# Thirteen of 24 normalizations moved to GpSimd in an attention-plus-gated-MLP kernel whose order is written out by hand

## The chip, the core and the metric

The kernel runs on one core of a Trainium2 chip. The core has TensorE (matrix products; in the profile PE, and PEld for the loading of its stationary operand), VectorE (DVE), ScalarE (ACT), GpSimd (POOL) and SyncE (SP, which here only issues DMAs). The four compute engines and the DMA queue run independently, each through its own instruction list in order, and wait for each other through semaphores. SBUF is the on-chip memory, PSUM holds eight banks of TensorE results; GpSimd does not read PSUM in this kernel.

The metric is the time of one execution in microseconds, as the device measures it. A profiled execution gives, beside its time, the span from the first to the last instruction and a trace of every instruction.

## The reference: what is computed

Two parts follow each other. The first is linear attention with decay over 4 batches, 8 heads, 768 positions and 64 columns a head, in blocks of 64 positions:

```python
intra = np.einsum('bhic,bhjc->bhij', qb, kb) * Dmask[None]
intra = np.einsum('bhij,bhjd->bhid', intra, vb)
inter = np.einsum('bhid,bhde->bhie', qb * lam_pow[None], kv_state)
out[:, :, sl] = intra + inter
kv_state = lam_block[None, :, None, None] * kv_state + np.einsum('bhsd,bhse->bhde', kb_dec, vb)
```

Its output, with the heads side by side, is x (4 x 768 x 512). The second part is a gated MLP with a spatial product over the 768 positions:

```python
h = np.maximum(x @ w_in, 0.0)
u, v = (h[..., :d_ff // 2].copy(), h[..., d_ff // 2:].copy())
v_n = (v - mu) / np.sqrt(var + 1e-06)          # mu, var over the 512 columns of v
v_s = np.einsum('ts,bsd->btd', w_spatial, v_n) + b_spatial[None, :, None]
gated = u * v_s
return (gated @ w_out).astype(np.float32)
```

Inputs and the output are float32; the products run in bfloat16.

## The kernel before

The 768 positions of a batch are cut into three steps of 256, so there are twelve steps, 0 to 11; batch b has steps 3b to 3b+2. There are no loops over time in the program: a string ORDER of 717 tokens is read from left to right, and each token issues the instructions of one operation. A token is a name, its numbers and the engine: T is TensorE, D VectorE, A ScalarE, P GpSimd, S the DMA queue of SyncE. `VN.7.1.P` normalizes the second half of step 7 on GpSimd. Only the order of the tokens of one engine among themselves matters, since each engine works off its own list; last numbers of many tokens name PSUM banks. Dependencies (data, and buffers that become free) are turned into semaphore waits by the framework.

One step n goes through these operations:

- Loads: LQ, LK, LV bring 512 KB each of q, k, v into one of three input buffers.
- Scaling: QM and KM multiply halves of q and k by powers of the decay into bfloat16 (line 331), VC and VD cast v.
- Transposes of q and k: by TensorE for steps 0 to 5 (TQ, TK, line 366, copied out of PSUM by EQ, EK), by transposing DMAs on the queue for steps 6 to 11 (DQ line 348, DK line 344).
- Attention: SC makes the scores (line 396), MK masks them into SBUF on VectorE (401), KP adds to the running state (425), SX, SY, SA copy and add state (431 to 441), AV makes the output (459, 468) in two parts. Between the parts stands FN, a copy of one element that keeps the second part behind the first. EX copies the result out as xT, the MLP's input.
- The v half: PV (493, four matmuls), EV with the ReLU (498, 500), BN the statistics (508, 509), RA the square root on ScalarE, RD the reciprocal and RB a product on VectorE, VN the normalized v_n (526 to 533). RB is needed only by ScalarE's form of VN.
- The u half: PU (544, eight matmuls) and EU with the ReLU.

When the three steps of a batch have their v_n and u, the spatial product follows: GP writes the bias into a PSUM bank, PW adds the product of v_n and the transposed W_spatial (570, six matmuls over the six 128-row pieces s of the batch; v_n of step n and half c is piece 2(n mod 3) + c), GM multiplies by u (576), PO and PH make the output product (581, 590), EO and EH copy it to SBUF, ST and SH store it.

The weights arrive in float32 during the first 45 us through staging buffers: WH and CW, CX for w_in; WQ (load of one 128-row piece), WC (cast), WT (six transposes on TensorE), EW (copy out of PSUM) for W_spatial; WP and WX for w_out. The staging buffers of w_in are used again: WQ.0 and WQ.1 wait for CW, WQ.4 and WQ.5 for CX. FL are matmuls of ones that fill TensorE's waits at the start; LB, LN, LL, LX make the table of decays; BB and BE spread the bias.

VN takes its engine from the token:

```python
def v_n(e, n, c):
    t, p2 = 2 * (n % NR) + c, n // NR % 2
    if e == "A":
        nc.scalar.activation(out=vn[p2][:, t], in_=vh[p2][:, t], func=AF.Identity,
                             scale=rstd[p2][:, t:t + 1], bias=nmr[p2][:, t:t + 1])
        return
    vec(e).tensor_scalar(out=vn[p2][:, t], in0=vh[p2][:, t], scalar1=mv[p2][:, t, 0:1],
                         scalar2=rstd[p2][:, t:t + 1], op0=ALU.subtract, op1=ALU.mult)
```

Of the kernel before, what the change touches and what calls it, by code (L numbers as in the profile page):

```python
# [17 lines left out]
one.D row.D FL.1.256.3.1.T FL.2.256.0.1.T FL.1.256.1.1.T LB.0.T FL.2.256.1.1.T FL.1.256.1.1.T FL.2.256.2.1.T
FL.2.256.5.1.T BB.1.6.T BB.0.1.T LN.0.A LL.D LX.A KM.0.1.D QM.0.0.P FL.1.256.0.1.T TQ.0.0.4.T QM.0.1.D KM.0.0.D
TQ.0.1.3.T TK.0.0.2.T TK.0.1.5.T FL.2.256.0.1.T EQ.0.0.4.D mkc.D EQ.0.1.3.D EK.0.1.5.D QM.1.1.D QM.1.0.P BE.0.1.A  # L20
BE.1.6.A EK.0.0.2.A tab.1.A SC.0.0.1.2.T MK.0.0.1.2.D VC.0.P KP.0.4.T SC.0.1.5.6.T TQ.1.0.0.T KM.1.0.P KM.1.1.P
# [60 lines left out]
EH.3.5.0.0.D ST.1.4.S SH.3.5.0.S ST.2.5.S GM.3.3.0.6.D GM.3.0.0.2.D PO.3.0.1.T PH.3.5.1.3.T PO.3.2.0.T EH.3.5.1.3.A
SH.3.5.1.A PO.3.1.6.T EO.3.1.6.A EO.3.3.5.D ST.3.3.S EO.3.4.4.D ST.3.4.S EO.3.0.1.D ST.3.0.S EO.3.2.0.D ST.3.2.S
ST.3.1.S
"""


# [556 lines left out]
```

## Time and profile before

| what | value |
|---|---|
| median of 3 runs | 143.06 us (142.86 to 143.22) |
| the profiled execution | 142.01 us |
| its span, first to last instruction | 140.3 us |
| mean granted TensorE clock | 0.995 |
| busy: TensorE / VectorE / ScalarE / GpSimd | 132.7 / 114.3 / 80.1 / 55.6 us |
| read from and written to HBM | 24.38 MB, 6.29 MB |

The profiled execution has 1.7 us around its span. "Busy" is the union of an engine's instructions; matmuls are pipelined and their ends modelled, so a busy TensorE row is not one at its peak. A row of the chain of waits is: start, length, what; a row of the timeline is: start, length, engine, line, operation, what is written and read, shape, count, and in brackets the idle time before it with what ended it. In the groups by line, the two numbers behind the bar are the busy time of the group and the mean nanoseconds of one instruction. L12 is line 12 of the kernel.

### The profile page before, as it was taken

The page shows a single profiled execution, that of the slowest core. Times are in us where ns is not written, and L with a number is a line of the kernel's source. Part 1 is how long each engine was busy: PE and PEld are TensorE (multiplying, and loading weights), DVE is VectorE, ACT ScalarE, POOL GpSimd, SP SyncE. Part 2 cuts the span into 40 slices and gives each one's busy share as a digit, 9 for nine tenths or more (in the row PEclk, how much of TensorE's full clock was granted, in tenths as well). Part 3 has the DMA queues.
Part 4 walks back from the last instruction along what each step waited for, and adds up shares of the span by engine and source line. Part 5 has one row for each costly group of instructions (what it writes and reads, how often), then busy time and mean ns, then how long its engine had stood idle before and what let it go on. Part 6 is the DMA issues. An engine that isn't in the chain of part 4 may idle for free.

```text
span 140.3 us, 4712 instructions
## 1 busy us (share of the span) xinstructions
PE 132.7 (95%) x1984; PEld 86.4 (62%) x1998; DVE 114.3 (81%) x229; ACT 80.1 (57%) x160; POOL 55.6 (40%) x64
## 2 busy tenths in 40 slices
PE   5999799999999999999999999999999999999990
PEld 3478574778567657648656456586555645866540
DVE  2299799979999998999488799779899799986660
ACT  4168488799667577359532278696124476962011
POOL 5268655842397459800861409701930000000000
PEclk9999999999999999999999999999999999999998
DMA  3999999999999999998917799999986980000174
GB/s 79 346 346 347 386 376 345 336 374 360 361 349 322 297 314 289 335 201 196 276 27 67 170 343 310 328 193 200 287 281 79 355 315 12 0 2 0 41 296 186
DMA packets 56729, 34.12 MB, mean 243 GB/s; under 512 B 13827, under 2 KB 51971, under 8 KB 56708
## 3 DMA queue, kind: packets, MB, share of 16 engines
q1 hardware_dynamic: 56560, 33.69, 84.4%
q8 instruction: 15, 0.25, 0.7%
q10 hardware_dynamic: 148, 0.13, 0.3%
q14 instruction: 6, 0.05, 0.1%
HBM read 24.38 MB, written 6.29 MB: 219 GB/s over the span
## 4 chain that ended last, share of the span: by engine, by line
PE 78%; SPq 6%; DMA 5%; DVE 3%; ACT 2%; issue 2%; POOL 1%; ACTq 0%; POOLq 0%
PE ps L570 22%; PE ps L581 14%; PE ps L493 14%; PE ps L544 13%; SPq L196 6%; DMA q_in<-in_q_dram 5%; PE ps L468 4%; PE ps L396 3%; PE ps L459 3%; PE ps L425 2%; PE ps L366 2%; POOL qc L331 1%; DVE vn L532 1%; ACT uT L498 1%; PE ps L556 1%
## 5 line engine op out<-in xcount | busy, mean ns | idle before, releaser
L570 PE MATMUL ps<-wt_sb,vn 128*128 128x384 bf16 x192 | 33.2, 326 | 0.2 <-DVE vn L532 0.2
L401 DVE TENSOR_TENSOR a_sb<-ps,m 128x1024 bf16<-128x1024 f32 x24 | 28.7, 1216 | 1.8 <-PE ps L396 1.3
L570 PEld LDWEIGHTS <-vn 128*128 128x128 bf16 x192 | 18.3, 98 | 12.1 <-DVE vn L532 0.6
L331 POOL TENSOR_TENSOR qc<-q_in,lqn 128x512 bf16<-128x512 f32 x18 | 19.4, 1093 | 15.4 <-DMA q_in<-in_q_dram 7.9
L544 PE MATMUL ps<-xT,win_sb 128*128 128x256 bf16 x192 | 23.1, 273 | 0.0
L493 PE MATMUL ps<-win_sb,xT 128*128 128x512 bf16 x92 | 22.5, 379 | 0.3 <-issue 0.2
L581 PE MATMUL ps<-wout_sb,gT 128*128 128x512 bf16 x82 | 21.3, 380 | 0.6 <-issue 0.2
L576 DVE TENSOR_TENSOR gT<-ps,uT 128x384 bf16<-128x384 f32 x32 | 16.7, 550 | 5.7 <-PE ps L570 5.6
L544 PEld LDWEIGHTS <-win_sb 128*128 128x128 bf16 x192 | 18.4, 98 | 3.9
L331 POOL TENSOR_TENSOR kc<-k_in,lv 128x512 bf16<-128x512 f32 x18 | 19.3, 1090 | 3.0 <-DMA k_in<-in_k_dram 2.6
L181 ACT ACTIVATE o_sb<-ps 128x512 f32<-128x512 f32 (+1 forms) x16 | 9.2, 580 | 17.4 <-PE ps L581 9.9
L508 DVE BATCH_NORM_STATS2 st<-vh 128x6 f32<-128x512 bf16 x24 | 16.4, 684 | 1.5 <-ACT vh L498 1.2
L181 ACT ACTIVATE ps<-bsp 128x384 f32<-128x384 f32 x23 | 11.1, 488 | 8.4 <-DVE gT L576 7.6
L181 ACT ACTIVATE xT<-ps 128x512 bf16<-128x512 f32 x23 | 12.5, 592 | 5.3 <-PE ps L468 5.1
L493 PEld LDWEIGHTS <-xT 128*128 128x128 bf16 x96 | 9.0, 98 | 9.5 <-ACT xT L181 1.3
L581 PEld LDWEIGHTS <-gT 128*128 128x128 bf16 x92 | 8.5, 98 | 9.1
L185 POOL CAST vb<-v_in 128x1024 bf16<-128x1024 f32 (+1 forms) x9 | 8.4, 941 | 12.6 <-DMA v_in<-in_v_dram 5.8
L498 ACT ACTIVATE vh<-ps 128x512 bf16<-128x512 f32 x18 | 10.5, 593 | 3.2 <-PE ps L493 3.2
L396 PE MATMUL ps<-qT,kT 64*64 64x128 bf16 x384 | 10.0, 226 | 1.1 <-issue 1.1
L468 PE MATMUL ps<-a_sb,vb 64*64 64x128 bf16 x384 | 9.9, 217 | 0.0
L498 ACT ACTIVATE uT<-ps 128x512 bf16<-128x512 f32 x16 | 9.2, 589 | 0.3 <-PE ps L544 0.3
L396 PEld LDWEIGHTS <-kT 64*64 64x64 bf16 x384 | 6.9, 111 | 2.8 <-issue 2.3
(77 smaller groups left out, 171.3 us busy)
## 6 DMA issues: line engine op xcount, KB each, us to landing
q_in<-in_q_dram SPq DMA_DIRECT2D x12, 512.0 KB, 6.7
k_in<-in_k_dram SPq DMA_DIRECT2D x12, 512.0 KB, 6.5
v_in<-in_v_dram SPq DMA_DIRECT2D x12, 512.0 KB, 6.3
out_dram<-o_sb SPq DMA_DIRECT2D x23, 256.0 KB, 3.1
wst<-in_moe_w_in_dram SPq DMA_DIRECT2D x4, 512.0 KB, 8.4
wst<-in_moe_w_spatial_dram SPq DMA_DIRECT2D x4, 384.0 KB, 7.4
wst<-in_moe_w_out_dram SPq DMA_DIRECT2D x1, 1024.0 KB
wss<-in_moe_w_spatial_dram SPq DMA_DIRECT2D x2, 384.0 KB, 7.0
```

The source lines that it names most:

```text
L181: nc.scalar.activation(out=o, in_=i, func=AF.Copy)
L331: vec(e).tensor_tensor(out=dst[n % NCA][:, u].rearrange("p u m o d -> p o (u m) d"), in0=src[n % NIN].rearrange("p (o u) m d -> p o u m d" ...
L396: nc.tensor.matmul(out=pa[o][row(c), w, j], lhsT=kT[n % NTR][row(o), u, j, c * Q64:(c + 1) * Q64], rhs=qv(n, o, u, c), start=(w == 0 and j ...
L401: nc.vector.tensor_tensor(out=a_sb[n % NA][:, i].rearrange("p o w j x -> p o w (j x)"), in0=ps[:, b0:b1 + 1:b1 - b0].rearrange("p o (w y) ...
L468: nc.tensor.matmul(out=po[c ^ o][row(w), c, i], lhsT=vb[n % NCA][row(c), 4 * o + u, j, :], rhs=a[row(c), i, o, w, j, :], start=(r == 0 and ...
L493: nc.tensor.matmul(out=bank(b), lhsT=x[:, slot(c, g)], rhs=win_sb[:, g, DH:DFF], start=(g == 0), stop=(g == NCH - 1))
L498: nc.scalar.activation(out=o, in_=i, func=AF.Relu)
L508: nc.vector.bn_stats(out=st6[p2][:, t], in_=vh[p2][:, t])
L544: nc.tensor.matmul(out=pu[:, f2].rearrange("p (c x) -> p c x", c=2), lhsT=win_sb[:, g, f * P:(f + 1) * P], rhs=x[:, slot(0, g):slot(1, g) ...
L570: nc.tensor.matmul(out=bank(b)[:, 0:HW], lhsT=vn[bb % 2][:, s, f * P:(f + 1) * P], rhs=wt_sb[:, s, i * HW:(i + 1) * HW], start=False, stop ...
L576: nc.vector.tensor_tensor(out=gT[bb % 2][:, f, cols], in0=bank(b)[:, 0:HW], in1=uT[bb % 2][:, f, cols], op=ALU.mult)
L581: nc.tensor.matmul(out=bank(b), lhsT=gT[bb % 2][:, f, t * P:(t + 1) * P], rhs=wout_sb[:, f, :], start=(f == 0), stop=(f == NCH - 1))
```

## The change

Only the string ORDER differs; the functions are the same. The new string has the same 717 operations.

- Engines of VN: before 18 on VectorE and 6 on ScalarE; after 13 on GpSimd, 7 on VectorE, 4 on ScalarE. On GpSimd are VN.1.0 and 1.1 (batch 0), 3.0, 4.0 and 4.1 (batch 1), 6.0, 6.1, 7.0 and 7.1 (batch 2), 9.0, 9.1, 10.0 and 10.1 (batch 3).
- Other operations that change engine, as counts before and after. EK: ScalarE 6 to 2, VectorE 3 to 7. EQ: ScalarE 6 to 8, VectorE 3 to 1. EV: ScalarE 18 to 15. EU: ScalarE 16 to 18. EO: ScalarE 15 to 17. EW: ScalarE 4 to 2. CW: ScalarE 2 to 0, VectorE 1 to 2, GpSimd 1 to 2. CX: one of two from GpSimd to VectorE. KM: GpSimd 18 to 20. VD: GpSimd 2 to 0, ScalarE 0 to 2.
- Loads: v of step 0 is third (before: q of step 1). WQ.1, 0, 2, 3, 4, 5 follow each other; before, LV.3 stood between WQ.5 and WQ.3. LQ.3 stands ahead of WH.2. LK.8 and LV.7 are behind the first four transposing DMAs instead of ahead of them.
- The order of every engine is another one, TensorE's included: of U groups, AV, KP and PO most are shifted by a few places, and many PSUM banks have other numbers. The fillers are 32 in both; one now stands behind the last output product.

The lines that hold the front, the spatial product of batch 0 and that of batch 2 (cut):

```diff
-lam.A BR.A tab.0.A LQ.0.S LK.0.S LQ.1.S LV.0.S LK.1.S LV.1.S LK.2.S LQ.2.S WH.0.S WH.1.S posk.P msk.P idn.P eps.D
...
-TQ.2.0.5.T FL.1.256.0.1.T TQ.2.1.1.T SA.1.1.D MK.1.1.3.4.D EQ.2.0.5.D CW.0.D SA.1.0.D EK.2.1.6.A EK.2.0.2.A
-AV.1.0.6.3.T SC.2.0.4.5.T MK.2.0.4.5.D EQ.2.1.1.A LV.2.S WH.3.S WH.2.S LK.3.S FN.1.6.3.A CW.1.A SC.2.1.0.1.T
-AV.1.1.6.3.T CW.3.A PV.0.0.2.T PV.0.1.4.T CX.1.P MK.2.1.0.1.D EV.0.1.4.D EX.1.0.6.A EX.1.1.3.A PV.1.0.5.T PV.1.1.0.T
...
-RA.2.A EW.2.0.1.D RD.2.D VN.1.1.D VN.1.0.D VN.0.0.D VN.2.1.D VN.2.0.D EW.0.0.2.A EW.1.0.4.A PU.2.0.0.T WQ.5.S LV.3.S
...
-RA.7.A EV.8.0.1.A SY.9.3.A RD.7.D RD.6.D SX.9.D RB.6.D BN.8.0.D PV.8.1.0.T RB.7.D EO.1.2.5.A EV.8.1.0.A VN.7.1.D
-BN.8.1.D VN.7.0.A VN.6.0.A PU.7.1.6.T PU.8.1.3.T RA.8.A EU.7.1.6.A RD.8.D RB.8.D VN.6.1.D SA.9.1.D VN.8.1.A VN.8.0.D
...
+lam.A BR.A tab.0.A LQ.0.S LK.0.S LV.0.S LQ.1.S LK.1.S idn.P posk.P msk.P one.D row.D FL.2.256.3.1.T FL.1.256.2.1.T
...
+VD.1.0.A SY.0.5.D MK.0.1.3.4.D EK.1.0.1.D SA.0.1.D EK.1.1.0.D FL.1.256.5.1.T SC.1.0.4.5.T AV.0.0.6.2.T
...
+WH.1.S FL.1.256.5.1.T TK.2.0.4.T FL.2.256.5.1.T FL.2.256.5.1.T TQ.2.0.5.T EX.0.0.6.A EX.0.1.2.A MK.1.1.0.1.D
+AV.1.0.1.0.T TQ.2.1.6.T TK.2.1.2.T EQ.2.0.5.A FN.1.1.0.A LV.2.S SY.1.3.D EK.2.0.4.D SA.1.0.D EK.2.1.2.D eps.D
+AV.1.1.1.0.T SC.2.0.3.4.T CW.2.D CW.3.D EQ.2.1.6.A SC.2.1.5.6.T SA.1.1.D MK.2.1.5.6.D EX.1.0.1.A EX.1.1.0.A WH.3.S
+MK.2.0.3.4.D CX.1.D CW.1.P CW.0.P LQ.3.S WH.2.S LK.3.S WQ.1.S WQ.0.S WQ.2.S PV.0.1.2.T PV.0.0.0.T PV.1.1.1.T
...
+EU.1.0.3.D RD.1.D PU.0.0.6.T TK.3.2.1.T WC.2.A EU.0.0.6.A WQ.3.S WQ.4.S WQ.5.S LK.4.S LV.3.S LQ.4.S EK.3.2.1.D
+WT.2.0.3.T WT.0.0.5.T WT.1.0.6.T EW.0.0.5.D EW.1.0.6.D PU.2.0.1.T VN.0.0.A RA.2.A EW.2.0.3.A EU.1.1.0.A RD.2.D
+VN.2.1.D VN.2.0.D WC.4.A EU.2.0.1.A WC.3.D WC.5.D WP.S LV.4.S VN.1.0.P VN.1.1.P SC.3.1.5.6.T PW.0.3.0.4.T
+PW.0.0.0.2.T MK.3.1.5.6.D GM.0.3.0.4.D KM.4.1.P KM.4.0.P QM.4.0.P GP.0.1.0.0.A GP.0.2.0.1.A WT.1.1.3.T PW.0.1.0.0.T
+WT.0.1.5.T EW.1.1.3.A WT.2.1.4.T GM.0.0.0.2.D GP.0.3.1.6.D EW.0.1.5.D EW.2.1.4.D GM.0.1.0.0.D VC.3.A GP.0.1.1.2.A
+GP.0.2.1.0.D PW.0.2.0.1.T WX.1.P GM.0.2.0.1.D KP.3.3.T SC.3.0.4.5.T PW.0.1.1.2.T PW.0.2.1.0.T GP.0.0.1.1.A SY.3.3.A
...
+LK.10.S LV.10.S KM.9.0.P KM.9.1.P GN.5.0.P DK.9.S ST.0.0.S ST.1.4.S KM.10.1.P VC.9.P LQ.11.S LK.11.S LQ.10.S DQ.9.S
...
+MK.8.0.5.6.D BN.6.0.D AV.8.0.0.3.T EV.7.1.4.A FN.8.0.3.D KP.9.1.T AV.8.1.0.3.T EX.8.0.0.A BN.7.0.D BN.7.1.D
+EX.8.1.3.A BN.6.1.D PO.1.2.6.T PV.8.0.0.T PV.8.1.5.T PU.7.1.4.T RA.7.A EV.8.0.0.D RD.7.D GP.2.3.0.3.A SY.9.1.A
...
+PU.7.0.6.T PU.8.1.1.T PU.8.0.5.T GP.2.2.0.0.A RD.8.D RB.8.D VN.8.1.D GP.2.2.1.4.D RB.7.D VN.8.0.A EU.8.1.1.A
+SA.9.1.D EU.8.0.5.D RB.6.D VN.7.1.P VN.6.0.P VN.6.1.P VN.7.0.P PW.2.2.0.0.T GM.2.2.0.0.D GP.2.0.0.1.D EU.7.0.6.A
+PW.2.1.1.2.T GM.2.1.1.2.D GP.2.3.1.5.A GP.2.1.0.0.A GP.2.0.1.6.A KM.10.0.P KM.11.0.P DK.10.S QM.11.1.P QM.11.0.P
+QM.10.0.P PW.2.3.0.3.T QM.10.1.D DQ.10.S PW.2.1.0.0.T PW.2.0.0.1.T PW.2.2.1.4.T GM.2.1.0.0.D GM.2.3.0.3.D KM.11.1.P
...
```

More of the change, by code (lines that the diff above doesn't have):

```diff
@@ L16 @@
 ORDER = """
-lam.A BR.A tab.0.A LQ.0.S LK.0.S LQ.1.S LV.0.S LK.1.S LV.1.S LK.2.S LQ.2.S WH.0.S WH.1.S posk.P msk.P idn.P eps.D
[L18 to L21, printed above, removed]
@@ L82 @@
[L82 to L84 removed]
+lam.A BR.A tab.0.A LQ.0.S LK.0.S LV.0.S LQ.1.S LK.1.S idn.P posk.P msk.P one.D row.D FL.2.256.3.1.T FL.1.256.2.1.T
+FL.4.256.0.1.T FL.1.256.6.1.T LB.2.T FL.2.256.6.1.T FL.2.256.3.1.T LN.2.A FL.1.256.1.1.T BB.0.5.T BB.1.3.T mkc.D
+LL.D LX.A KM.0.1.P QM.0.1.D QM.0.0.D TQ.0.0.0.T TK.0.1.6.T KM.0.0.D TK.0.0.4.T TQ.0.1.2.T BE.0.5.D BE.1.3.A
```

100 lines of the change are left out of this document (46 added, 54 removed).

## The prediction

> **What bounds the kernel now.** I read the profile's page first, then the chain that ended last in order of time, then the timeline around the places where the chain leaves TensorE. On the page, the span, busy times, granted clock, DMA share and rate in 40 slices:
>
> ```profile
> span 140.3 us, 4712 instructions
> ...
> PE 132.7 (95%) x1984; PEld 86.4 (62%) x1998; DVE 114.3 (81%) x229; ACT 80.1 (57%) x160; POOL 55.6 (40%) x64
> ...
> PEclk9999999999999999999999999999999999999998
> DMA  3999999999999999998917799999986980000174
> GB/s 79 346 346 347 386 376 345 336 374 360 361 349 322 297 314 289 335 201 196 276 27 67 170 343 310 328 193 200 287 281 79 355 315 12 0 2 0 41 296 186
> ```
>
> The clock is granted in full, so TensorE's time is its work and its waits. The chain in order of time (start, length, what):
>
> ```profile
> 9.30 7.37 DMA q_in<-in_q_dram
> ...
> 16.80 2.05 POOL qc L331 x2
> ...
> 20.89 3.40 PE ps L493 x15
> ...
> 43.88 0.45 PE ps L366 x8
> ...
> 58.11 0.17 ACT seen L181
> ...
> 90.98 4.37 PE ps L544 x40
> 95.35 5.85 PE ps L570 x36
> ...
> 136.73 0.60 ACT o_sb L181
> ```
>
> Until 16.8 us the chain waits for inputs (q of step 2 is the eighth load), GpSimd scales that q, and from the first V projection at 20.89 until 136.73 the chain is TensorE with small interruptions. The work is fixed: 0.109 us a U matmul (4.37 / 40), 0.1625 us a spatial one (5.85 / 36), 0.056 us a transpose (0.45 / 8). GpSimd is busy for 40% and VectorE for 81%, but neither sets the end. So taking v_n from VectorE (11 of them) and ScalarE (2) is worth only the TensorE waits that it ends. There are two candidates: the start of the V projections and the start of the spatial product. Behind them I allow nothing: the pause at 58.11 (a fence copy after AV.5.0) is still there, since again only KP stands between AV.5.0 and AV.5.1. The tail behind the last matmul (140.3 - 136.73 = 3.6 us) has the same last copy and the same last store; the filler matmul behind the last output product keeps nobody waiting.
>
> **The change part by part, first the front.** The timeline before the first V projection:
>
> ```profile
> 18.89 0.40 PE L366 MATMUL ps<-ident,qc 128*128 128x128 bf16 x4
> ...
> 19.09 0.42 DVE L183 CAST win_sb<-wst 128x512 bf16<-128x512 f32 x1
> 19.22 0.75 POOL L185 CAST win_sb<-wst 128x512 bf16<-128x512 f32 x1 [0.38 <-DMA wst<-in_moe_w_in_dram]
> ...
> 19.33 0.60 ACT L181 ACTIVATE qT<-ps 128x512 bf16<-128x512 bf16 x1 [0.22 <-PE ps L366]
> ```
>
> The view of DMA issues has, as the last column, the median us from issue to landing:
>
> ```profile
> v_in<-in_v_dram SPq DMA_DIRECT2D x12, 512.0 KB, 6.3
> ...
> qT<-qc SPq DMA_TRANSPOSE x6, 3.3
> ```
>
> The ten loads up to w_in's second V piece are the same set in both orders, so GpSimd's QM.2 pair (16.80 + 2.05 = 18.85) and TQ.2.1 (18.89) stay where they are. After that, before: AV.1.0, SC.2.0, the wait for EQ.2.1 (19.33 + 0.60 = 19.93), SC.2.1, AV.1.1, then PV. Changed: AV.1.0 is ahead of TQ.2.1, and TK.2.1 and AV.1.1 lie inside the wait for EQ.2.1. TK.2.1 starts 4 x 0.056 behind TQ.2.1 and, at 0.40 long like it, ends about 19.55; VectorE copies it (EK.2.1, about 0.4 as its cast at 19.09) until 20.0, SC.2.0 and SC.2.1 follow, and PV.0.1 can begin at 20.4: 0.45 us gained. The casts must keep up: GpSimd makes CW.1 and CW.0 from 18.85 (2 x 0.75, until 20.35), VectorE CW.2 and CW.3 from 20.0 (2 x 0.42, until 20.85; their data was there at 19.22, when GpSimd's cast stopped waiting); the matmul that reads CW.3 comes 3 x 0.22 behind 20.4, at 21.05. Bounds: 0.6 gained (PV right behind the copies) to 0.2 lost (casts late); I take 0.45.
>
> **The spatial product's start.** The timeline there, and one row of 20 us (ScalarE's last two casts):
>
> ```profile
> 19.88 1.13 ACT L181 ACTIVATE win_sb<-wst 128x512 bf16<-128x512 f32 x2
> ...
> 33.57 2.19 DVE L532 TENSOR_SCALAR vn<-vh,mv,rstd 128x512 bf16<-128x512 bf16 x5
> ...
> 34.43 0.87 POOL L185 CAST wsp_raw<-wst 128x768 bf16<-128x768 f32 x1 [2.47 <-DMA wst<-in_moe_w_spatial_dram]
> ...
> 34.81 0.82 PE L570 MATMUL ps<-wt_sb,vn 128*128 128x384 bf16 x4
> ...
> 35.82 2.45 PE L570 MATMUL ps<-wt_sb,vn 128*128 128x384 bf16 x14 [0.19 <-DVE vn L532]
> ```
>
> Four matmuls run, the fifth waits: it could begin at 34.81 + 4 x 0.1625 = 35.46 and begins at 35.82, because VectorE makes five v_n in a row at the end (33.57 + 2.19 = 35.76). Changed: ScalarE makes v_n 0 and 1, GpSimd 2 and 3, VectorE 4 and 5. With the PE order 0.45 earlier, PW.0.3.0 is reached at 34.35. The same fifth matmul, which now needs VN.2.0 from VectorE, is due at 35.0. VectorE has taken on CX.1, one more cast of w_in and several PSUM copies (EK.2, EQ.3, EW.1.0) in this stage and given away four v_n, EV.0.0 and QM.3.1; adding its row durations from 20.0 on I get VN.2.0 done at about 34.6. So 0.36 is saved, and the next thing late is VN.2.0 itself with 0.4 in hand. Bounds: 0 (VectorE's queue 0.4 later than my sum) to 0.36; I take 0.36.
>
> What GpSimd needs for one v_n, no row shows. Its nearest rows:
>
> ```profile
> 1.82 0.64 POOL L234 TENSOR_SCALAR_AFFINE_SELECT mfull<-mfull 128x512 bf16<-128x512 bf16 x1
> ...
> 12.92 1.16 POOL L185 CAST vb<-v_in 128x512 bf16<-128x512 f32 x2
> ...
> 14.05 1.48 POOL L331 TENSOR_TENSOR kc<-k_in,lv 128x512 bf16<-128x512 f32 x1
> ```
>
> and in the groups by line those of v_n itself and of GpSimd's two-input product:
>
> ```profile
> L331 POOL TENSOR_TENSOR kc<-k_in,lv 128x512 bf16<-128x512 f32 x18 | 19.3, 1090 | 3.0 <-DMA k_in<-in_k_dram 2.6 <-PE ps L468 0.5
> ...
> L532 DVE TENSOR_SCALAR vn<-vh,mv,rstd 128x512 bf16<-128x512 bf16 x18 | 7.0, 431 | 0.0
> ...
> L529 ACT ACTIVATE vn<-vh,nmr,rstd 128x512 bf16<-128x512 bf16 x6 | 4.7, 816 | 0.0
> ...
> L500 DVE TENSOR_SCALAR vh<-ps 128x512 bf16<-128x512 f32 x6 | 4.0, 681 | 1.1 <-PE ps L493 1.1
> ```
>
> One input of 512 elements costs 0.58 to 0.64, two cost 1.09 and 1.48 at worst. v_n has one large input, so I take 0.64 and keep 1.48 as the other end. In batch 0 the two GpSimd v_n follow WC.0 and RD.1 (about 31.5 in my sum of VectorE's queue): even 2 x 1.48 ends at 34.5, and the fourth matmul is due at 34.85. KM.4 and QM.4 are queued behind them; their products are first transposed by TK.4 and TQ.4 beyond 42 us.
>
> **The later batches.** Batch 1's GpSimd v_n have over 3 us between RD.4 and PW.1; batch 3's start at RD.9 and RD.10, with two V and four or more U groups (5 us) ahead of PW.3. Batch 2 is the tight one: four in a row (7.1, 6.0, 6.1, 7.0) behind RD.7 and RD.6, which the new order puts after BN.6.0, 7.0, 7.1, 6.1 and EV.8.0.
>
> ```profile
> 85.35 1.21 DVE L401 TENSOR_TENSOR a_sb<-ps,m 128x1024 bf16<-128x1024 f32 x1
> ...
> 91.28 0.69 DVE L508 BATCH_NORM_STATS2 st<-vh 128x6 f32<-128x512 bf16 x1
> ...
> 92.00 0.18 DVE L509 BATCH_NORM_AGGREGATE mv<-st 128x2 f32<-128x6 f32 x1
> ```
>
> In times of before: MK.8 ends at 86.56, four BN of 0.82 (92.00 - 91.28, and 0.1 until the next) and a fence copy take VectorE to about 90.0, EV.8.0 (0.68) to 90.7, and the two reciprocals let GpSimd start at 90.95. PV.8.1, five U groups and then PW.2 at 95.35 are unchanged in place; the fourth v_n (7.0) is read by the third matmul, due at 95.68. At 0.64 GpSimd ends at 93.5; up to 1.18 each nothing waits. Behind them on GpSimd wait KM.10.0, KM.11.0, QM.11 and QM.10.0, so the transpose DMA DQ.10 goes at about 93.5 + 5 x 1.04 = 98.7:
>
> ```profile
> 85.25 3.04 POOL L331 TENSOR_TENSOR qc<-q_in,lqn 128x512 bf16<-128x512 f32 x3
> ...
> 105.69 0.41 PE L396 MATMUL ps<-qT,kT 64*64 64x128 bf16 x16
> ```
>
> Before, QM.10.0 was in the first row; its reader SC.10 is near 105, 6 us behind the new issue, and a transpose into qT lands 3.3 us after its issue. Covered.
>
> **Loads.** v of step 0 third makes VC.0 about 1.5 us earlier and q of step 1 as much later; QM.1 is not last there, k of step 1 is (same place). LQ.3 before WH.2 delays CX.0 by one load (1.5 us), whose reader PU.1.0 comes at about 29.5 against 26.7. The six spatial pieces in a row put LV.3 behind WQ.3, WQ.4 and LK.4 as well: 1.3 MB at 350 GB/s is 3.7 us.
>
> ```profile
> 25.04 0.44 SPq L196 DMA_DIRECT2D v_in<-in_v_dram  x1
> ...
> 34.76 1.06 ACT L181 ACTIVATE vb<-v_in 128x1024 bf16<-128x1024 f32 x1
> ```
>
> v3 was issued at 25.04 and, by the median of 6.3 us, there at 31.3; now 35.0. Its cast VC.3 follows EW.1.1 on ScalarE, about 37.3 to 38.4; KP.3, behind four spatial groups and three WT (34.35 + 4 x 0.975 + 18 x 0.056 = 39.25), does not wait. If v3 came only at 34.76, the latest that the row allows, it would wait 0.3. I take none.
>
> **Sum.** Gains 0.45 + 0.36. I charge 0.2 for SC.3.0, due at 39.5, which now needs EW.2.1 at the end of a VectorE queue that I add up to 39.4 with an error as large as that. Together 0.6: the profiled run of 142.01 becomes 141.4. The median of the runs, 143.06, stands 1.05 above that execution; the forecast on it is 142.4. Faster than 142.63 or slower than 143.49 is what 0.3% means here, about what a measurement of this kernel can tell from no change.
>
> **Rivals.**
> 1. Slower: GpSimd's v_n is slow and PW.2 waits for it. It decides from 1.18 us each; at 1.48 the chain ends at 90.95 + 5.9 = 96.9, 1.2 late, so -0.6 + 1.2: 143.7, and above 1.48 more. For it: two scalars per partition and two arithmetic steps, which no row has. Against: one-input rows are half of that. Chance 0.17.
> 2. Slower: KP.9 waits on GpSimd. There VC.9 now stands behind KM.10.1, which needs k of step 10, loaded behind DQ.8 and a store:
>
> ```profile
> 84.25 1.04 POOL L185 CAST vb<-v_in 128x1024 bf16<-128x1024 f32 x1 [5.57 <-DMA v_in<-in_v_dram]
> ...
> 87.33 0.42 PE L425 MATMUL ps<-vb,kc 64*64 64x64 bf16 x32
> ```
>
> Now the second load behind DQ.8 lands at 84.25; if k10 lands as late as that or a microsecond later, 84.25 + 1.0 + 2.08 = 87.3 is the point from which KP.9 waits, and each microsecond more costs one: 143.5 with one, 144.5 with two. Against: it is the first load there. Chance 0.13.
> 3. No change: PV's start is held by something I do not see (the last cast, 19.88 + 1.13 = 21.01 before), and the new VectorE queue eats the 0.36: 143.0. Chance 0.15.
> 4. The two engines get in each other's way at the front. Overlapping casts at 19.09 and 19.22 took 0.42 and 0.75, GpSimd's at 12.92 0.58 each: sharing has cost 0.17. If one had to wait out the other, CW.3 would stand behind VC.2 (1.04) on GpSimd and PV.0's fourth matmul slip by 0.8: 143.2. Chance 0.10. The Trainium skill, SBUF — State Buffer, section Who interferes with whom, says that a VectorE cast in a two-port mode and a GpSimd instruction exclude each other for the whole instruction. By that rule this rival holds; the overlapping rows at 19.09 and 19.22 do not show such an exclusion.
>
> **How the numbers follow.** My forecast has 0.45, its own range 141.8 to 142.8. Faster: most of it, 0.42. Same: rivals 3 and 4 without their tails and the forecast's upper edge, 0.23. Slower: rivals 1 and 2 and tails, 0.35. The range, 141.7 to 144.1, holds the forecast, the bounds of the front (0.6 and 0.36 without the charge: 142.1, less 0.4 for pauses I counted nowhere) and the two slower cases up to their middle.
>
> **What would show it.** Right: the first V projection at 20.3 to 20.5, the first spatial matmul at 34.2 to 34.6 with no wait at its fifth, GpSimd v_n rows of 0.6 to 0.8, no TensorE wait on GpSimd at PW.2 or KP.9, and a last matmul about 0.6 earlier. Wrong: v_n on GpSimd above 1.18; TensorE waiting for VectorE or ScalarE copies between 36 and 66 us, where ScalarE now copies more q and output and VectorE more k; or DMA rows landing later than before.

## The result and the profile after

The changed kernel takes 151.58 us (median; 150.68 to 152.22) against 142.99 us of the kernel before, timed on the same chip: the ratio is 1.0595, 95% interval 1.0538 to 1.0651. Ratios, here and below, are of undisturbed executions alone, which are three of six for vn_copy. The forecast was 142.4 us, with a range up to 144.1. The profiled execution took 152.22 us, with a span of 150.5 us (before: 142.01 and 140.3). These two are the longest and a short execution of their kernels, so their spans differ by 10.2 us where the medians differ by 8.6. The page of the changed kernel:

```profile
span 150.5 us, 4722 instructions
...
PE 135.7 (90%) x1984; PEld 86.9 (58%) x1998; DVE 114.8 (76%) x224; ACT 77.2 (51%) x153; POOL 82.6 (55%) x76
...
PEclk9999999999999999999999999995999999999998
...
PE 55%; POOL 16%; DVE 10%; SPq 5%; DMA 5%; issue 2%; ACT 2%; POOLq 1%; DVEq 0%; ACTq 0%
...
L569 PE MATMUL ps<-wt_sb,vn 128*128 128x384 bf16 x192 | 35.5, 335 | 6.8 <-POOL vn L531 6.8
L531 POOL TENSOR_SCALAR vn<-vh,mv,rstd 128x512 bf16<-128x512 bf16 x13 | 27.1, 2091 | 19.3 <-DVE rstd L517 19.2
```

GpSimd is busy for 27 us more, and its v_n takes 2.09 us, where VectorE's took 0.43. The line of the chain's shares has GpSimd at 16%; the spatial matmuls (line 569) waited 6.8 us for it. The granted clock has a hole near 102 us. The chain of waits in order of time, in the changed kernel, its pieces on GpSimd (start, length, what):

```profile
32.38 1.93 POOL vn L531
34.45 2.17 POOL vn L531
...
65.37 4.28 POOL vn L531 x2
...
93.86 1.94 POOL vn L531
95.92 6.19 POOL vn L531 x3
...
125.86 4.13 POOL vn L531 x2
...
132.05 2.06 POOL vn L531
```

In every batch the chain now goes through GpSimd's v_n. TensorE's timeline in the changed kernel shows what each costs (in brackets the idle time and its releaser):

```profile
20.28 3.63 PE L492 MATMUL ps<-win_sb,xT 128*128 128x512 bf16 x15
...
34.89 0.66 PE L569 MATMUL ps<-wt_sb,vn 128*128 128x384 bf16 x3
36.67 1.64 PE L569 MATMUL ps<-wt_sb,vn 128*128 128x384 bf16 x9 [1.11 <-POOL vn L531]
...
50.97 1.02 PE L580 MATMUL ps<-wout_sb,gT 128*128 128x512 bf16 x3 [1.04 <-DVE ysb L436]
...
68.67 0.65 PE L569 MATMUL ps<-wt_sb,vn 128*128 128x384 bf16 x3
69.70 4.56 PE L569 MATMUL ps<-wt_sb,vn 128*128 128x384 bf16 x27 [0.37 <-POOL vn L531]
...
98.05 0.34 PE L569 MATMUL ps<-wt_sb,vn 128*128 128x384 bf16 x1
100.10 0.34 PE L569 MATMUL ps<-wt_sb,vn 128*128 128x384 bf16 x1 [1.72 <-POOL vn L531]
102.16 6.99 PE L569 MATMUL ps<-wt_sb,vn 128*128 128x384 bf16 x34 [1.72 <-POOL vn L531]
...
131.45 0.49 PE L569 MATMUL ps<-wt_sb,vn 128*128 128x384 bf16 x2
132.11 0.34 PE L569 MATMUL ps<-wt_sb,vn 128*128 128x384 bf16 x1 [0.17 <-POOL vn L531]
134.16 5.54 PE L569 MATMUL ps<-wt_sb,vn 128*128 128x384 bf16 x33 [1.72 <-POOL vn L531]
```

In the kernel before, the products of batches 1 to 3 run without a wait:

```profile
66.61 5.04 PE L570 MATMUL ps<-wt_sb,vn 128*128 128x384 bf16 x30
...
95.18 6.01 PE L570 MATMUL ps<-wt_sb,vn 128*128 128x384 bf16 x36
...
123.54 6.01 PE L570 MATMUL ps<-wt_sb,vn 128*128 128x384 bf16 x36
```

Against before, the first spatial matmuls of batches 0 to 3 start at 34.89, 68.67, 98.05 and 131.45 us instead of 34.81, 66.61, 95.18 and 123.54. So the stages grew by 2.0, 0.8, 5.0 and 2.3 us (the last from 16.8 to 19.1), together with the 0.1 at the start the 10.2 us between the spans. Batch 2's product waits twice for 1.72 us, at 100.10 and at 102.16. By windows of 2 us (columns: length, then busy time and count of PE, PEld, DVE, ACT and POOL, then the granted clock, the DMA share and GB/s), the clock falls behind these waits:

```profile
100.00:102.00 2.00, 0.34 (x1) 0.10 (x1) 0.00 (x0) 0.00 (x0) 2.00 (x2) 0.85 0.47 176
102.00:104.00 2.00, 1.84 (x6) 0.89 (x7) 0.34 (x1) 0.00 (x0) 2.00 (x3) 0.50 0.02 6
104.00:106.00 2.00, 2.00 (x11) 1.14 (x10) 1.34 (x4) 0.91 (x2) 2.00 (x3) 0.80 0.58 131
```

TensorE stands idle in nearly all of the first window, so only the clock missing from the other two costs time: the 34 matmuls behind the second wait take 6.99 us instead of 34 x 0.1625 + 0.17 = 5.70 (0.17 is what a row lasts beyond its matmuls' shares), 1.3 us more. 2 x 1.72 + 1.3 = 4.7 us are most of the 5.0 of batch 2's stage. In batch 3, one wait of 1.72 us left the clock alone: its 33 matmuls take 5.54 us, as at full clock.

### The profile page after: what moved, and what is told of

The parts are those of the page before. It is cut to its first block, busy times and chain, and to the rows that moved or that the text cites. A ratio compares the mean times of both kernels' runs of the same rounds, so it can differ in the third digit from the quotient of the medians.

```text
span 150.5 us, 4722 instructions
## 1 busy us (share of the span) xinstructions
PE 135.7 (90%) x1984; PEld 86.9 (58%) x1998; DVE 114.8 (76%) x224; ACT 77.2 (51%) x153; POOL 82.6 (55%) x76
## 4 chain that ended last, share of the span: by engine, by line
PE 55%; POOL 16%; DVE 10%; SPq 5%; DMA 5%; issue 2%; ACT 2%; POOLq 1%; DVEq 0%; ACTq 0%
PE ps L569 20%; POOL vn L531 15%; PE ps L580 11%; PE ps L492 10%; SPq L195 5%; DMA q_in<-in_q_dram 5%; DVE st L507 3%; PE ps L395 3%; PE ps L467 3%; PE ps L543 2%; PE ps L458 2%; PE ps L424 1%; POOLq L638 1%; POOL qc L330 1%; DVE kc L330 1%
## 5 line engine op out<-in xcount | busy, mean ns | idle before, releaser
L569 PE MATMUL ps<-wt_sb,vn 128*128 128x384 bf16 x192 | 35.5, 335 | 6.8 <-POOL vn L531 6.8
L531 POOL TENSOR_SCALAR vn<-vh,mv,rstd 128x512 bf16<-128x512 bf16 x13 | 27.1, 2091 | 19.3 <-DVE rstd L517 19.2
L330 POOL TENSOR_TENSOR kc<-k_in,lv 128x512 bf16<-128x512 f32 x20 | 21.3, 1080 | 6.5 <-DMA k_in<-in_k_dram 4.0
L330 POOL TENSOR_TENSOR qc<-q_in,lqn 128x512 bf16<-128x512 f32 x17 | 18.6, 1104 | 9.3 <-DMA q_in<-in_q_dram 9.3
L180 ACT ACTIVATE o_sb<-ps 128x512 f32<-128x512 f32 (+1 forms) x19 | 10.7, 570 | 21.4 <-PE ps L580 12.9
L180 ACT ACTIVATE ps<-bsp 128x384 f32<-128x384 f32 x24 | 11.6, 495 | 14.1 <-DVE gT L575 11.5
L184 POOL CAST vb<-v_in 128x1024 bf16<-128x1024 f32 x8 | 8.9, 1114 | 14.1 <-issue 5.4
L497 ACT ACTIVATE uT<-ps 128x512 bf16<-128x512 f32 x18 | 10.5, 596 | 1.9 <-PE ps L543 1.9
L497 ACT ACTIVATE vh<-ps 128x512 bf16<-128x512 f32 x15 | 8.7, 590 | 4.9 <-PE ps L492 4.6
```

Source lines behind the costliest of these rows:

```text
L180: nc.scalar.activation(out=o, in_=i, func=AF.Copy)
L330: vec(e).tensor_tensor(out=dst[n % NCA][:, u].rearrange("p u m o d -> p o (u m) d"), in0=src[n % NIN].rearrange("p (o u) m d -> p o u m d" ...
L497: nc.scalar.activation(out=o, in_=i, func=AF.Relu)
L569: nc.tensor.matmul(out=bank(b)[:, 0:HW], lhsT=vn[bb % 2][:, s, f * P:(f + 1) * P], rhs=wt_sb[:, s, i * HW:(i + 1) * HW], start=False, stop ...
```

## The experiments

Theory A: the price of a v_n on GpSimd makes the loss, through the waits of the spatial products. Theory B: the new orders and loads lose time themselves. Theory C: VectorE and GpSimd slow each other down. A ratio below is always to the kernel before on the same chip, with its 95% interval. Line numbers shift a little from kernel to kernel.

### What one v_n costs on GpSimd

```diff
+ ZP.1.P      # at the end: on GpSimd alone, tensor_scalar with two, one or no scalars by pointer,
+             # 256, 512, 1024 elements, bf16 and f32; tensor_tensor; tensor_copy
+ ZP.0.P, ZP.2.P   # the first from 103 us on; four v_n behind ZP.1 and a row on VectorE (cut)
```

> The kernel before with extra work into buffers that nothing reads any more, so its time is not meant to be compared: GpSimd runs single instructions of many forms, once from 103 us beside a busy VectorE, once after the last output column is copied, with every other engine idle, and then four v_n beside a row of two-input instructions on VectorE. Theory A1, the price is the form's own (a tensor_scalar on GpSimd is slow by element): v_n 128x512 takes 2.07 us in the quiet stretch too, half of it at 256 elements, twice at 1024, and a tensor_tensor of the same size takes about 0.75. Theory A2, it is the reading of two scalars by pointer: the same with constants is much shorter, and with one pointer about half. Theory C, it is VectorE's work beside it: in the quiet stretch v_n takes 1.0 us or less, and 2 or more beside VectorE.

Groups by line on GpSimd in the stretch behind the last output copy, with all other engines idle:

```profile
L616 POOL TENSOR_SCALAR wsp_raw<-vh,mv,rstd 128x512 bf16<-128x512 bf16 x2 | 4.1, 2068 | 0.1
L620 POOL TENSOR_SCALAR wsp_raw<-vh,mv,rstd 128x1024 bf16<-128x1024 bf16 x1 | 3.8, 3778 | 0.1
...
L623 POOL TENSOR_SCALAR wsp_raw<-vh 128x512 bf16<-128x512 bf16 x1 | 1.9, 1927 | 0.1
L622 POOL TENSOR_SCALAR wsp_raw<-vh,mv 128x512 bf16<-128x512 bf16 x1 | 1.6, 1560 | 0.1
...
L619 POOL TENSOR_SCALAR wsp_raw<-vh,mv,rstd 128x256 bf16<-128x256 bf16 x1 | 1.2, 1219 | 0.1
...
L628 POOL TENSOR_TENSOR wsp_raw<-vh,mv 128x512 bf16<-128x512 bf16 x1 | 1.0, 1038 | 0.1
...
L627 POOL COPY wsp_raw<-vh 128x512 bf16<-128x512 bf16 x1 | 0.6, 609 | 0.1
```

A1 holds: 2.07 us alone, the price is the form's own; only its 0.75 for a tensor_tensor was missed (1.04). From 256 to 1024 elements it is (3778 - 1219) / 768 = 3.3 ns an element and some 0.4 us. A copy takes 0.61, a tensor_scalar of one arithmetic step 1.56, of two 2.07; with constants in place of pointers (line 623) it is hardly shorter, 1.93, and a float32 input takes the same 2.07. Two tensor_tensor (2 x 1.04) would be no cheaper. The Trainium skill, GPSIMD Engine Reference, section 4.1 Engine selection, calls a one-input instruction on GpSimd "roughly line-rate"; the copy is not far from that (0.61 us, beside 0.42 of VectorE's cast of 512 elements at 19.09 us in the kernel before), the v_n is far from it: it has one large input and takes five times VectorE's 0.41.

The same instructions from 103 us on, beside the kernel's work, were meant as the other half. They read rstd ahead of its next reciprocal in program order and so held the kernel up by 34 us: VectorE was idle there too, and that half tells nothing. Nor do the four v_n meant to run beside a row on VectorE, which started only when that row had ended; the kernel contend, below, has the two engines beside each other.

### The v_n back to VectorE and ScalarE

vn_back puts all 13 back, at other places; vn_back2 and vn_back3 place them better:

```diff
- VN.1.0.P VN.1.1.P VN.3.0.P VN.4.0.P VN.4.1.P VN.7.1.P VN.6.0.P VN.6.1.P VN.7.0.P VN.9.1.P VN.9.0.P VN.10.0.P VN.10.1.P
+ (vn_back) RD.2.D VN.1.0.D VN.1.1.D ... EU.6.1.0.A VN.7.0.A VN.6.0.A ... EU.9.1.4.A VN.9.0.A ... RA.11.A VN.10.0.A, the others .D
+ (vn_back2) RD.1.D VN.1.0.D EK.3.2.1.D EW.0.0.5.D VN.1.1.D ... BN.11.0.D VN.9.0.D VN.9.1.D ... RD.11.D VN.10.1.D VN.10.0.D
+ (vn_back3) as vn_back2, each batch in the order of reading, and SY.4.2.D KM.5.1.D KM.5.0.D instead of KM.5.1.D KM.5.0.D ... SY.4.2.D
```

> The changed kernel with its 13 v_n taken back from GpSimd (nine to VectorE, four to ScalarE, at the places in batches 0 to 3 at which their inputs are ready); all else of the new orders and loads stays. Theory A, the price of a v_n on GpSimd (2.07 us beside 0.41 on VectorE) makes the loss: the waits of the first spatial matmuls go (1.5 + 0.4 + 3.8 + 2.2 us by the chain), with them the stretch at half clock behind them, and 143 us or less is left, at most 144 with VectorE's longer queue. Theory B, the new orders and the new row of loads make the loss themselves: it stays above 147 us. Theory C, VectorE and GpSimd slow each other down where KM.5 runs beside QM.5: only 1.0 us of the loss stays in any case, as a wait for ysb at 51 us.

Measured: 146.88 us, ratio 1.0241 (1.0180 to 1.0302), between A's 144 at most and B's 147 at least. More than half of the loss is gone, but not all, and the trace showed new waits of my own making: 1.5 us for VectorE's v_n in batch 0 (four v_n in 2.81 us beside GpSimd's KM.4) and 0.9 us for a bias that ScalarE wrote late in batch 3.

> The changed kernel with all 13 v_n taken back from GpSimd, as in the kernel vn_back (146.88 us), but the two of batch 0 right behind the reciprocal of their step, ahead of two evictions on VectorE, and batch 3's four all on VectorE, so that ScalarE writes the biases ahead of its products in time. Theory A (the price of a v_n on GpSimd makes the loss, and what was left in vn_back came of where the v_n were put back): its waits for v_n in batch 0 (1.5 us), the stretch of reduced clock behind them (1.7 us by the granted clock of 0.95 over 35.0 us) and the wait of 0.9 us for a bias in batch 3 go, and 142.6 to 144.0 us are left. Theory B (the new orders and loads lose time themselves): it stays at 145.5 us or above.

Measured: 144.73 us, ratio 1.0147 (1.0108 to 1.0185). A's range was missed by 0.7 us, B's by 0.8.

> As the kernel vn_back2 (144.73 us: the changed kernel with all v_n on VectorE and ScalarE), with the v_n of each batch in the order in which the products read them, and with the two KM of step 5 behind the addition into ysb on VectorE, ahead of which they stood. If the 2.1 us that vn_back2 still loses to the kernel before are waits of the first spatial matmuls for a v_n that VectorE makes late (0.5 us in batch 0, some 0.2 to 0.4 in each other batch, by the length of the groups of 30 and 36 matmuls) and the wait of 0.6 us for ysb: 142.8 to 143.9 us. If the new orders lose it elsewhere: 144.4 us or more.

Measured: 145.05 us, ratio 1.0168 (1.0123 to 1.0214). The wait for ysb went, and TensorE now waits 1.0 us for kc at the transpose of step 5's k: one wait took the other's place, and by its expectation the new orders lose the rest elsewhere than in the two places named. So three quarters of the loss (0.045 of 0.060 in the ratio) go with the v_n; but VectorE, to which the change had given other work, is busy for 117 to 118 us in these kernels against 114.3 before, so they can't say whether the rest, some 2 us, is B's.

> The changed kernel with only the eight v_n of batches 2 and 3 taken back (four to VectorE and ScalarE each way as in vn_back2), the five of batches 0 and 1 left on GpSimd. Theory A: the waits of 3.8 us and 2.2 us and the half clock of about 1.4 us go, those of batches 0 and 1 (1.3 and 0.4 us) and the 1.0 us for ysb stay: 144 to 145 us. If the time lost at the front (in batch 0) is what counts and the later waits only take up slack that other work would have needed, it stays above 147 us.

Edit: as vn_back2 for batches 2 and 3 only. Measured: 145.26 us, 0.3 above A's range; the ratio of 1.0187 (1.0139 to 1.0235) overlaps vn_back2's. So the five v_n on GpSimd in batches 0 and 1 cost half a microsecond by the medians, which can't be told from nothing, and the eight of batches 2 and 3 make most of the loss.

### The same 13 v_n in the kernel before

```diff
- VN.1.1.D VN.1.0.D VN.4.0.D VN.4.1.D VN.3.0.D VN.7.1.D VN.7.0.A VN.6.0.A VN.6.1.D VN.9.0.A VN.10.1.D VN.9.1.D VN.10.0.A
+ the same at the same places, each with .P
```

> The kernel before with the same 13 v_n given to GpSimd in place, all orders as they were. Theory A: slower by 6 to 11 us (149 to 154), the waits for v_n in the same four places, batch 2 and batch 3 the largest. Theory B: 143 to 145, since the old orders carry it. Were the price 2.07 us only beside the changed kernel's load, the v_n would show other durations here.

Measured: 172.49 us, ratio 1.2063 (1.2008 to 1.2118): 29 us slower, where A expected 6 to 11. The timelines of GpSimd and, in the last row, of TensorE:

```profile
106.45 1.04 POOL L329 TENSOR_TENSOR qc<-q_in,lqn 128x512 bf16<-128x512 f32 x1 [7.70 <-DMA qT<-qc]
...
111.46 8.26 POOL L530 TENSOR_SCALAR vn<-vh,mv,rstd 128x512 bf16<-128x512 bf16 x4
...
117.72 0.50 PE L568 MATMUL ps<-wt_sb,vn 128*128 128x384 bf16 x1 [14.61 <-POOL vn L530]
```

In the old order batch 2's v_n stand behind step 11's q and k on GpSimd, and these wait for a transposing DMA to release their buffer. The price is one part of this loss, the place in GpSimd's list another, and the runs don't say how much each makes; the changed kernel's order has the v_n ahead of that work.

### Price against slack

Two of batch 3's v_n in the kernel before, then four, to GpSimd, idle there since 103 us:

```diff
- VN.9.0.A ... VN.9.1.D            (slack4 also: VN.10.1.D ... VN.10.0.A)
+ RD.9.D VN.9.0.P VN.9.1.P         (slack4 also: RD.10.D VN.10.0.P VN.10.1.P)
```

> The kernel before with two of batch 3's v_n alone (step 9's) given to GpSimd, right behind the reciprocal of step 9, which ends at 118.68 us there; GpSimd has been idle since 103 us. Theory A (a wait only where the price of 2.07 us a piece passes the slack): the two are done by 118.7 + 4.2 = 122.9 us, ahead of the first spatial product of batch 3 at 123.54 us, so the time is that of before, within 0.4 us. If a v_n on GpSimd costs time by itself (VectorE slowed beside it, by the pairings measured after the end): up to 0.5 us slower.

Measured: ratio 0.9997 (0.9967 to 1.0028). Two v_n within the slack cost nothing, and bring nothing.

> As the kernel slack, but all four v_n of steps 9 and 10 on GpSimd. Theory A: the fourth is done at 118.7 + 4 by 2.08 = 127.0 us; its matmul would have started at 123.54 + 3 by 0.1625 = 124.03 us, so TensorE waits 3.0 us in batch 3, and the time is 2.6 to 3.4 us above before, up to 4.5 if the granted clock falls behind the waits as it did in batch 2 of the changed kernel. If other work of the stage takes up the wait: under 2 us.

Measured: 147.71 us, ratio 1.0363 (1.0310 to 1.0416), which is 5.2 us and above the 4.5 expected at most. The timelines of GpSimd and TensorE:

```profile
118.78 8.28 POOL L530 TENSOR_SCALAR vn<-vh,mv,rstd 128x512 bf16<-128x512 bf16 x4 [15.89 <-DVE rstd L516]
...
125.05 0.34 PE L568 MATMUL ps<-wt_sb,vn 128*128 128x384 bf16 x1 [1.03 <-POOL vn L530]
127.11 6.82 PE L568 MATMUL ps<-wt_sb,vn 128*128 128x384 bf16 x33 [1.72 <-POOL vn L530]
```

The fourth ends at 127.06, as worked out. 33 matmuls then take 6.82 us instead of the 5.54 of the same 33 in the changed kernel's batch 3: the clock fell again (0.59 and 0.56 by windows of 2 us from 126 to 130 us), and 2.75 + 1.3 = 4.1 of the 4.4 us between the spans (144.7 and 140.3) are explained.

### Other prices in the changed kernel

Three kernels leave the changed kernel's orders as they are and put another GpSimd instruction in the place of v_n:

```diff
+ if e == "P":   # vn_copy: tensor_copy of one rstd element, then of v; vn_mult: tensor_tensor, v times rstd; vn_scale: tensor_scalar, v times rstd
```

> The changed kernel with its 13 GpSimd v_n replaced by a plain copy of v (0.61 us) behind a copy of one element of rstd (0.18 us), so that they still wait for rstd; the normalization of these 13 is left out. Price 0.8 us a piece, near the 0.64 that the prediction took. Theory A (the price alone makes the loss, by the waits it causes): no wait for v_n is left; of the 151.58 us go 7.8 of waits and 1.4 of half clock: 142.0 to 143.0 us. Theory B (the new orders lose about 2 us by themselves): 144.3 us or more.

> As vn_copy, with one multiplication by rstd as a two-input instruction (1.04 us) in place of the v_n; the subtraction of the mean is left out. Theory A with the slack read in the changed kernel's trace: batch 2's four start at 93.86 us and the fourth is wanted at 98.05 + 2 by 0.1625 = 98.4 us, so the threshold is 4.5 / 4 = 1.13 us (the prediction had 1.18): no wait yet, 142.0 to 143.2 us. Theory B: as for vn_copy, 144.3 or more.

> As vn_copy, with one multiplication by rstd as a one-operation tensor_scalar (1.56 us) in place of the v_n; the subtraction of the mean is left out. Theory A: batch 2's fourth is done at 93.86 + 4 by 1.57 = 100.1 us, 1.7 us late, batches 0 and 3 are late by 0.2 and 0.3 us, and the clock may fall for a microsecond: 144.0 to 146.0 us. If there were no threshold and the price counted by itself, it would lie at about two thirds of the way from vn_copy to the changed kernel, near 148.

| kernel | price of one, us | ratio |
|---|---|---|
| vn_copy | 0.18 + 0.60 | 1.0129 (1.0083 to 1.0174) |
| vn_mult | 1.04 | 1.0167 (1.0123 to 1.0211) |
| vn_scale | 1.57 | 1.0239 (1.0196 to 1.0282) |
| the changed kernel | 2.09 | 1.0595 (1.0538 to 1.0651) |

There is a threshold: from 0.8 to 1.57 the ratio rises by 0.011, from 1.57 to 2.09 by 0.036. The first two have no wait for GpSimd's v_n; vn_scale waits 0.28 and 1.21 us in batch 2, of the 1.7 expected, and not in batches 0 and 3, where 0.2 and 0.3 were. But even the cheapest is 1.3% (1.8 us) slower than before, where A had 143 at most. B is right for that part. TensorE's waits in vn_copy that before does not have, or has shorter (0.19 us in the place of the first):

```profile
36.24 1.47 PE L572 MATMUL ps<-wt_sb,vn 128*128 128x384 bf16 x8 [0.42 <-DVE vn L534]
...
97.59 2.62 PE L572 MATMUL ps<-wt_sb,vn 128*128 128x384 bf16 x14 [0.81 <-ACT vn L527]
100.83 3.08 PE L572 MATMUL ps<-wt_sb,vn 128*128 128x384 bf16 x18 [0.62 <-ACT ps L179]
```

VectorE's last v_n of batch 0, ScalarE's of batch 2 and a bias that ScalarE writes come late: 1.85 us by these rows, of 2.7 us between the profiled spans (143.0 and 140.3). The trace also shows what makes the first two late. The rows around ScalarE's v_n, whose second factor nmr is the product RB on VectorE:

```profile
94.63 2.03 POOL L329 TENSOR_TENSOR kc<-k_in,lv 128x512 bf16<-128x512 f32 x2
...
95.05 1.64 DVE L521 SCALAR_TENSOR_TENSOR nmr<-mv,rstd 128x2 f32<-128x2 f32 x1
...
96.72 0.81 ACT L527 ACTIVATE vn<-vh,nmr,rstd 128x512 bf16<-128x512 bf16 x1 [1.65 <-DVE nmr L521]
```

RB takes 0.13 to 0.16 us elsewhere and 1.64 us here, until GpSimd's KM.10.0 and KM.11.0 are done. In the kernel before, GpSimd stands idle at that place, from 90.3 to 97.8 us. In batch 0, VectorE's two v_n take 1.48 us (from 34.71) instead of 0.8, beside KM.4. So theory C makes two of the three waits. This was read from the trace, not tried by moving these instructions.

### The front, the clock, and two engines side by side

front_after takes the changed kernel's tokens up to `EV.1.0.5.A`, then those of before, with banks 3, 4, 6 renamed to 4, 6, 3; front_after2 renames only up to batch 0's products.

> The changed kernel's orders and loads up to the eviction of the first V projections (ScalarE's second of step 1), and from there the orders of the kernel before, with the banks renamed so that both halves agree; v_n all on VectorE and ScalarE. It keeps the step of the prediction that held (the first V projection at 20.3 instead of 20.9 us). If that gain is carried to the end: 142.3 to 142.7 us against 143.0. If it is lost in a queue behind it (as the prediction's third rival has it): 142.9 to 143.2. If the seam of the two orders costs more than it brings: slower.

Measured: 148.14 us, ratio 1.0391 (1.0355 to 1.0427). The renaming had set pairs of banks apart that MK reads as one view (`ps[:, b0:b1 + 1:b1 - b0]`), and TensorE waited for a_sb throughout.

> As the kernel front_after (the changed kernel's orders and loads up to the eviction of the first V projections, the orders of before from there), but the banks are renamed only up to batch 0's spatial products, so that every pair of banks that the mask instruction reads at once lies side by side again, as in both kernels; front_after had pairs that lie apart, and waits for the masked scores in every batch. If these pairs made its 148.14 us, it is now 142.2 to 143.4 us, and the gain of 0.55 us at the first V projection is either kept (142.2 to 142.6) or lost in a queue (142.6 to 143.4). If the seam makes it: above 146 us still.

Measured: 142.76 us, ratio 1.0012 (0.9984 to 1.0040). So the renamed banks of the later batches made the 148, by waits for a_sb; the reason, most likely that the view spans the bank in between and waits for it, wasn't tried. The first V projection starts at 20.50 instead of 20.89 us, and the first U product then waits 0.78 us for VectorE's v: the gain is lost at the seam, and whether another order could keep it stays open.

> The changed kernel with 14 matmuls of 128x256 into a part of bank 7 that nothing reads, ahead of the second and of the third matmul of batch 2's first spatial product, to fill the two waits of 1.72 us for v_n (14 by 0.107 at full clock is 1.5 us). If the half clock from 102 to 104 us comes from TensorE's standing idle there, the granted clock stays at 1.00 from 100 to 106 us and the span is 1.0 to 1.8 us shorter, with the waits unchanged. If the clock falls for another reason (the chip's load), it falls again, and the time stays at 151 to 152 or grows.

```diff
+ if bb == 2 and f == 2 and i == 0 and s in (1, 2): f_x(e, 14, 256, ...)   # 14 matmuls ahead of the waiting one
```

Windows of 2 us, columns as above:

```profile
102.00:104.00 2.00, 1.81 (x13) 0.99 (x11) 0.72 (x2) 0.13 (x1) 2.00 (x3) 1.00 0.01 4
104.00:106.00 2.00, 2.00 (x15) 1.18 (x12) 1.91 (x3) 0.77 (x2) 2.00 (x3) 1.00 0.58 131
```

With TensorE kept busy the clock stays at 1.00: its standing idle made the hole. The span is 149.4 us instead of 150.5; the ratio of 1.0565 (1.0495 to 1.0635) can't be told from 1.0595.

> The kernel before with the changed kernel's share for step 5 alone: both KM on VectorE, both QM on GpSimd (before: both KM and one QM on GpSimd, one QM on VectorE). If the two-input instructions of both engines slow each other (0.69 to 1.33 us on VectorE, 1.04 to 1.31 us on GpSimd, as measured beside each other) and the addition into ysb waits behind them: 0.4 to 1.2 us slower than before, with a wait for ysb near 48 us. If the slowing is hidden: within 0.4 us.

Edit: `QM.5.1.P QM.5.0.P KM.5.1.D KM.5.0.D` behind `LK.5.S` in the kernel before. Measured: ratio 1.0018 (0.9994 to 1.0041), no wait for ysb. But both QM ran alone, from 42.85 to 44.89 us, before the KM at 46.15: the collision of the changed kernel did not take place, so this says only that the share by itself is harmless. There it did:

```profile
47.43 2.60 POOL L330 TENSOR_TENSOR qc<-q_in,lqn 128x512 bf16<-128x512 f32 x2 [5.02 <-DMA q_in<-in_q_dram]
47.60 2.98 DVE L330 TENSOR_TENSOR kc<-k_in,lv 128x512 bf16<-128x512 f32 x2
```

These are the changed kernel's rows ahead of its wait of 1.04 us for ysb. The price of such a meeting was measured behind the kernel's end:

> The kernel before with work added after its last output column is copied, into buffers that nothing reads any more, so that its time is not meant to be compared: GpSimd and VectorE each run v_n and the two-input multiplication of KM, first alone and then beside each other in the four pairings. If GpSimd's v_n is slow because of VectorE beside it, it takes more than 2.07 us there. If the two-input instructions of the two engines get in each other's way (the collision of KM.5 and QM.5 at 47 us in the changed kernel, 1.49 us and 1.30 us each), KM on VectorE takes 0.65 alone and about 1.3 to 1.5 beside GpSimd's. If the slow ones there came of a loading queue or of other things, both keep their times of alone.

Edit: rows of each instruction on each engine behind the last output copy. Groups by line in stretches with VectorE alone, and beside GpSimd's two-input row; then VectorE's and GpSimd's two-input rows beside each other:

```profile
L609 DVE TENSOR_SCALAR wsp_raw<-vh,mv,rstd 128x512 bf16<-128x512 bf16 x14 | 5.8, 412 | 0.5
...
L609 DVE TENSOR_SCALAR wsp_raw<-vh,mv,rstd 128x512 bf16<-128x512 bf16 x6 | 6.6, 1094 | 0.2
...
L329 DVE TENSOR_TENSOR kc<-k_in,lv 128x512 bf16<-128x512 f32 x7 | 9.3, 1328 | 0.2
...
L329 POOL TENSOR_TENSOR qc<-q_in,lqn 128x512 bf16<-128x512 f32 x6 | 7.9, 1314 | 0.4
```

VectorE's v_n goes from 0.41 to 1.09 us beside GpSimd's two-input instructions, its KM from 0.67 at the shortest to 1.33 (a mean of seven, of which the first ran ahead of GpSimd's row; the others take 1.41 or more); GpSimd's two-input one goes from 1.04 to 1.31 beside KM. GpSimd's v_n takes 2.07 us alone, 2.40 beside VectorE's v_n, 2.56 beside its KM, and 2.09 in the changed kernel. So theory C is a real effect, but not the cause of the price. By the rows shown, it is behind the wait for ysb and, in vn_copy, behind two of the three waits that the new orders make; neither was tried by itself.

## Why the prediction was wrong

**The step that failed is "What GpSimd needs for one v_n".** It was bounded by the rows of a one-input affine_select (0.64, taken) and of the slowest two-input product (1.48). It costs 2.07 us, outside both ends. The argument that v_n has one large input counted inputs alone; by the price run the form and its arithmetic steps count as well: 0.61 for a copy, 1.56 for a tensor_scalar of one step, 2.07 for one of two, where a two-input product of one step takes 1.04. Of the 0.0595 that the changed kernel loses, 0.0466 (some 6.7 us) go when the price falls to 0.78 us with the orders unchanged (vn_copy); the other 0.0129 (some 1.8 us) are the new orders' and were missed by other steps, below. Rival 1 had named "two arithmetic steps, which no row has" and got 0.17.

**The mechanism of rival 1 and its threshold held.** Batch 2 was the tight place; the threshold of 1.18 us agrees with the table of prices, since 1.04 causes no wait and 1.57 does. With the measured price its own sum, 90.95 + 4 x 2.08 = 99.3 against 95.68, would have given a wait of 3.6 us; 3.4 were measured. GpSimd started at 93.86, by about as much later as the product.

**Three places called safe were not, by the same price.** Batch 0: start 32.38 instead of 31.5 (0.6 of it is VectorE's RB, 0.75 us long at 28.67 beside GpSimd's KM.3), end 36.62 instead of 34.5 at most, wait 1.1. Batch 1 had 3 us for its last two and needed 4.3: wait 0.4. Batch 3: "5 us" of cover against 8.2: wait 1.9.

**What was not in the sum at all.** The clock behind broken waits (1.3 us in batch 2), the meeting of KM.5 and QM.5 with the wait of 1.04 us for ysb, and VectorE's short instructions held up beside GpSimd's products. The second was only listed as a sign of a wrong forecast (waits between 36 and 66 us); of the third, rival 4 had priced the casts at the front alone.

**The front.** The first V projection came at 20.28, a little earlier than forecast (20.4). But the first spatial matmul started at 34.89, not at 34.35, and its fifth would have waited for VectorE even without GpSimd (0.42 us in vn_copy). Of the gain of 0.61 us, 0.39 is left at the first U product (24.54 against 24.93) and nothing at 34.89. The step that failed here is the sum of VectorE's queue: VN.2.0, forecast for 34.6 us, is done at 35.7 (two v_n from 34.60 on in 1.08 us). So both gains of the sum, 0.45 and 0.36, did not arrive; rival 3 had the queue right, but not a late start of PV. With a price near the forecast one, the change would still have been some 1.3% slower (vn_copy), outside what was forecast.

**What held.** KP.9 (rival 2) and KP.3 did not wait, DQ.10 held nothing up though it went at 107.6 us instead of 98.7, and the pause and the tail are as before. Rival 4's effect exists, as contend and vn_copy show, but not at the place that it named. The Trainium skill's rule that the prediction cites for it (SBUF — State Buffer, Who interferes with whom) agrees with VectorE's v_n, of which each one beside GpSimd's row takes one GpSimd instruction's time (1.09 and 1.04 us); at the front no row shows it, since the V projections were not late.

## What to carry to other kernels

Price an instruction on another engine by a row of the same form there; if there is none, count its arithmetic steps as well as its inputs, and let the upper bound be open. In these runs, work moved to an idle engine is free up to the slack between its last input and its first reader (two v_n in 4.9 us cost nothing, four cost 3.6%), and only if nothing that waits stands ahead of it in that engine's list. Look also at what runs beside it on the other engine: RB on VectorE took 1.64 us instead of 0.15 beside two of GpSimd's products. And waits on TensorE of a few microseconds can cost more than themselves when the granted clock falls behind them.

## What the runs showed of the hardware

- GpSimd's tensor_scalar with two operations on bfloat16 takes about 3.3 ns an element and 0.4 us, five times VectorE's; two tensor_tensor of 1.04 us each, which could do the same work, add up to the same.
- Two idle stretches of 1.72 us with one matmul between them halved the granted clock for 3.4 us (101.4 to 104.8); matmuls of no use in the stretches kept it at 1.00. The holes of slack4 (waits of 1.03 and 1.72 us) and vn_back (0.43 and 1.03 us) are 3.4 us long too. Waits alone don't decide it: 1.24 and 1.72 us in batch 3 of before_vn_pool left the clock at 1.00, and what sets the difference wasn't tried.
- Beside a row of GpSimd's two-input instructions, VectorE's v_n takes 1.09 us instead of 0.41, while GpSimd's instructions keep their 1.04 us; where both engines run two-input instructions, both get longer (0.67 to 1.41 us and 1.04 to 1.31 us).
